# Sinkhorn-sorted attention with a gated MLP: the keys of two batches mixed in 64x64 blocks on four array tiles, and a new order of units

## The chip, the cores and the metric

The kernel runs on one core of a Trainium2 chip. The metric is the device time of one execution in microseconds (us), lower is better. Engines are named as the profile names them: PE is the matrix engine (PEld its weight loads), DVE the vector engine, ACT the scalar engine, POOL the GpSimd engine, SP the engine that here only issues transfers.

## The reference

Four batches of eight heads, 768 tokens, 64 features per head, in float32. An 8x8 matrix per head (`sort_net`) is normalised five times by exp, rows and columns; with it the eight blocks of 96 tokens of k and of v are mixed; each query block attends to its mixed block; then a gated MLP follows.

```python
for _ in range(5):
    P = P - np.max(P, axis=-1, keepdims=True)
    P = np.exp(P)
    P = P / (np.sum(P, axis=-1, keepdims=True) + 1e-09)
    P = P / (np.sum(P, axis=-2, keepdims=True) + 1e-09)
k_sorted = np.einsum('bhij,bhjcd->bhicd', P, k_b).reshape(B, H, S, D)
v_sorted = np.einsum('bhij,bhjcd->bhicd', P, v_b).reshape(B, H, S, D)
...
scores = scale * np.matmul(q_b, k_sb.transpose(0, 1, 2, 4, 3))
attn = softmax(scores)                      # per block of 96 tokens
x = np.matmul(attn, v_sb)                   # heads side by side: (4, 768, 512)
h = np.maximum(x @ w_in, 0.0)               # 512 -> 1024
u, v = h[..., :512], h[..., 512:]
v_n = (v - mu) / np.sqrt(var + 1e-06)
v_s = np.einsum('ts,bsd->btd', w_spatial, v_n) + b_spatial[None, :, None]
out = (u * v_s) @ w_out
```

## The kernel before, in words

The program is straight-line. It is built from small units, and a table of unit names (`ORDER`, L18 to L54) gives the order in which they are emitted; each engine then works through its own instructions in that order and waits at semaphores. A unit's fields are, where they apply, the PSUM bank (a digit from 0 to 3 is a pair of banks, 10 to 17 a single one), the engine that empties the bank (A for ACT, D for DVE, P for POOL), the batch, and the pair of heads or the tile of tokens. Eight banks of PSUM are shared by everything.

The units that matter here:

- `L:q`, `L:k`, `L:v` load one batch of q, k or v, `L:wv`, `L:wu`, `L:wsa`, `L:wsb`, `L:wo`, `BI` load weights and the bias. All are issued by POOL, and the transfers turn float32 into bfloat16. One partition holds six neighbouring tokens of a head, so 128 partitions hold a head.
- `SK` is one round of normalising; `PR` spreads the result over 128 partitions by matmuls (L267); `P0` and `PD` multiply it with a mask to the 128x128 matrix `pd` of each head (P times the identity of 16). `P0` makes the first batch's on DVE, `PD` the others' on POOL, four heads each. There are two buffers of `pd`.
- `KT` mixes and turns the keys of a pair of heads (L395): for each of six strips the keys (128 partitions x 64 features) are the weights and `pd` of the head (128 columns) moves; one head's result goes to the lower 64 partitions of PSUM and the other's to the upper 64. `VT` and `VB` do the like for v of the first batch; `VM` (L422) mixes v of the other batches, and `VC` copies them by transfers into blocks.
- `QT` turns the queries on PE (L326) in the first two batches; in the third and fourth `QP` copies a pair of heads on ACT or DVE (L375) and `QX` turns them by a transfer.
- `SC` (L454) makes the scores of a pair of heads for half of the blocks: 64 rows of the array for each head, then exp on ACT (L459). `AT` (L500) multiplies with the mixed v, and DVE divides (L507, L508). `XT` on PE or `XD` by a transfer (L518) turns the attention's result.
- `VP` and `VH` (L567) make the v half of the hidden layer, `ST`, `LN`, `LA` normalise it; `UP` (L613) the u half; `WT`, `WW` (L536, L543) turn the spatial weights; `SP` and, for the last batch, `SH` (L625, L681) apply them; `GT` and `GH` multiply by u on DVE or POOL; `OP`, `OE`, `OS` and at the end `OH`, `OI`, `OJ` are the output product, its copy out of PSUM and its store.
- `DM` are matmuls on zeros that fill PE's time at the start.

The batches overlap: while one is in the hidden layer, the next is in attention. A second, safe path for inputs out of range stands behind a branch that is not taken here.

Of the kernel before, what the change touches and what calls it, by code (L numbers as in the profile page):

```python
# [8 lines left out]
FP32 = mybir.dt.float32  # L9
# [10 lines left out]
QC:A:0 SK:3 SK:4 QC:A:1 QT:10:A:0:2 IV:2 QT:11:A:0:3 DM:12:4:512 QT:12:A:0:0 DM:13:10:192 PR:10 MB P0:0:2 P0:2:4  # L20
QT:11:D:0:1 VT:2:A:0:0 VT:3:D:0:1 PC:A P0:4:6 P0:6:8 VB:13:A:0:0 VB:12:D:0:1 L:k:0:0:8 VT:2:A:0:2 KT:3:D:0:1
KT:1:A:0:2 KT:0:A:0:3 VT:2:D:0:3 SC:3:0:1:1 KT:1:D:0:0 SC:0:0:2:0 VB:14:D:0:2 SC:3:0:3:0 L:k:1:0:8 AT:1:0:1:1
SC:0:0:0:0 L:v:1:0:8 PD:1:0:4 VB:15:D:0:3 SC:3:0:1:0 AT:1:0:2:0 SC:0:0:2:1 AT:2:0:3:0 SC:3:0:0:1 PD:1:4:8 AT:1:0:0:0
KT:0:A:1:0 XT:14:D:0:0:2 AT:3:0:0:1 SC:1:0:3:1 KT:0:A:1:3 AT:2:0:2:1 VM:1:A:1:0 AT:3:0:3:1 VM:0:A:1:1 VM:2:D:1:3
L:q:1:0:8 VM:1:A:1:2 XT:16:A:0:1:2 L:wv AT:0:0:1:0 XT:17:A:0:1:0 KT:2:D:1:1 KT:1:A:1:2 QT:16:D:1:1 QT:10:D:1:3
QT:11:A:1:2 QT:17:D:1:0 XT:14:D:0:0:0 SC:1:1:1:0 L:wsa SC:0:1:2:1 SC:3:1:2:0 VP:15:D:0:4 ST:0:4 VP:14:D:0:3 L:wu
SC:1:1:0:0 SC:0:1:1:1 VP:15:D:0:1 L:wsb ST:0:3 WT:16:A:1 WT:17:D:0 VP:14:A:0:0 ST:0:1 VH:15:A:0:2 ST:0:0 WT:16:A:2
VC:1:0:4 L:q:2:0:8 VH:17:A:0:5 VC:1:4:8 PD:2:0:4 ST:0:2 ST:0:5 AT:1:1:0:0 LN:0:0:6 AT:0:1:1:0 UP:2:A:0:0:0
UP:3:A:0:1:0 BI LA:0:3 LA:0:4 AT:1:1:2:0 SC:2:1:0:1 UP:0:A:0:1:1 LA:0:1 AT:3:1:2:1 L:v:2:0:8 WT:14:A:3 L:k:2:0:8
LA:0:5 LA:0:2 WW:1:D:4 LA:0:0 SC:0:1:3:1 SC:3:1:3:0 UP:2:A:0:0:1 PD:2:4:8 AT:0:1:3:1 QP:A:2:0 SP:1:0:3 QP:A:2:3  # L30
AT:3:1:3:0 QP:A:2:2 AT:2:1:0:1 QP:A:2:1 SP:0:0:0 AT:1:1:1:1 SP:3:0:2 VM:2:A:2:2 XD:1:0 VM:0:A:2:1 GT:D:0:0 SP:1:0:1
VM:3:D:2:0 GT:P:0:1 VM:2:A:2:3 VH:10:A:1:0 ST:1:0 KT:1:A:2:0 KT:2:D:2:1 KT:3:A:2:3 QX:2:0:4 KT:0:D:2:2 XD:1:1
UP:1:A:1:1:0 VH:16:D:1:1 SC:2:2:2:0 SC:0:2:0:0 VC:2:0:4:0:4 ST:1:1 GT:P:0:2 SC:1:2:3:0 VH:17:D:1:3 L:wo UP:2:A:1:1:1
AT:0:2:2:0 VH:16:A:1:4 AT:1:2:0:0 GT:P:0:3 VH:17:D:1:5 SC:2:2:1:0 L:q:3:0:8 SC:0:2:0:1 SC:1:2:1:1 VH:16:A:1:2 ST:1:3
UP:2:A:1:0:0 ST:1:5 AT:0:2:3:0 ST:1:4 ST:1:2 UP:1:A:1:0:1 LN:1:0:6 OP:3:0:2:2 LA:1:5 LA:1:1 SC:2:2:3:1 L:v:3:0:8
SC:0:2:2:1 PD:3:4:8 LA:1:0 OP:1:0:4:2 PD:3:0:4 LA:1:3 LA:1:2 OE:A:0:2 LA:1:4 L:k:3:0:8 QP:D:3:0 VC:2:4:8:0:4 OE:A:0:4
AT:2:2:3:1 SP:0:1:3 QP:A:3:3 AT:3:2:1:0 AT:1:2:2:1 QP:A:3:1 SP:2:1:1 AT:0:2:1:1 QP:A:3:2 VM:3:A:3:1 OP:1:0:0:2
OE:D:0:0 OS:0:0:0:1:A OS:0:0:1:2:A VM:2:A:3:3 AT:3:2:0:1 SP:0:1:2 VM:1:A:3:0 GT:P:1:1 XD:2:0 VM:3:D:3:2 SP:2:1:0
VH:16:D:2:2 QX:3:0:4 KT:0:A:3:0 KT:1:D:3:2 KT:2:D:3:3 KT:3:A:3:1 XD:2:1 VH:10:D:2:0 SC:1:3:0:1 ST:2:2 SC:3:3:0:0
SC:2:3:3:1 VC:3:4:8:0:4 OS:0:4:0:1 OS:0:4:1:2 VH:11:D:2:4 VH:10:A:2:5 AT:1:3:0:1 GT:P:1:3 VH:16:D:2:3 ST:2:3 ST:2:5  # L40
GT:P:1:2 SC:2:3:1:1 SC:0:3:2:1 SC:1:3:1:0 VH:17:A:2:1 GT:D:1:0 UP:2:A:2:1:0 AT:0:3:2:1 UP:1:A:2:1:1 ST:2:1 AT:3:3:1:1
ST:2:4 AT:2:3:3:1 UP:0:A:2:0:1 ST:2:0 UP:1:A:2:0:0 VC:3:0:4:0:4 AT:3:3:0:0 LN:2:0:6 LA:2:2 OP:0:1:0:2 OE:A:1:0 LA:2:4
AT:2:3:1:0 OP:1:1:4:2 LA:2:5 SC:3:3:2:0 LA:2:0 LA:2:3 LA:2:1 SC:0:3:3:0 OP:2:1:2:2 AT:3:3:3:0 SP:0:2:1 GT:D:2:1
# [25 lines left out]
def kernel(  # L69
# [18 lines left out]
    TB = 128 // NB  # L88
    BH = B * H
# [63 lines left out]
    prep_sb = const.tile([128, NB, BH], BF16, name="prep_sb")  # L153
    vm = const.tile([128, G, H, VW], BF16, name="vm")
# [8 lines left out]
    st = {}  # L163
# [7 lines left out]
    def u_L(what, *a):  # L171
        if what in ("q", "k", "v"):
# [113 lines left out]

    def u_PC(eng):
        copy(eng, prep_sb, st["pr"])
# [157 lines left out]
    def u_SC(ps, b, hp, ih):  # L446
# [3 lines left out]
        for ii in range(NI):  # L450
            i = ih * NI + ii
            for hh in range(2):
                rows = slice(hh * 64, hh * 64 + 64)
# [9 lines left out]
    def u_SM(b, hp, ih):  # L463
# [5 lines left out]
        for ii in range(NI):  # L469
            i = ih * NI + ii  # L470
            for hh in range(2):
                rows = slice(hh * 64, hh * 64 + 64)
# [203 lines left out]
    def u_SH(ps, b, mc, c):  # L676
        b, mc, c = int(b), int(mc), int(c)
        t, x = ps_tile(ps)[:, 0], tokens(c)
        w = x.stop - x.start
        for n in range(G):  # L680
            nc.tensor.matmul(  # L681
                t[:, 0:w], lhsT=st["v_sb", b, n][:, mc * 128:(mc + 1) * 128],
                rhs=wspT[:, x.start // 128:x.stop // 128, n, :],
                start=(n == 0), stop=(n == G - 1),
            )
# [74 lines left out]
    def general_path():  # L760
# [88 lines left out]
```

## Time and profile before

| | |
|---|---|
| time before | 150.09 us, median of 3 runs (149.42 to 150.87) |
| span of the profiled execution, first to last instruction | 147.7 us; its own device time is not given apart, the median of the runs is 2.4 us above its span |
| instructions | 4114 |
| PE / DVE / ACT / POOL busy | 141.4 / 115.1 / 85.2 / 39.1 us |
| first use of the loaded k (first mixing of keys) | 15.45 us |
| first matmul with `wu` (first `UP`) | 38.23 us |
| TensorE clock granted | 1.00 throughout |

A busy time is the union of the instructions of that engine. Times in the views count from the start of the span. In the chain of work that ended last, each piece is the time from the end of the piece before to its own end, so that a delay ahead of a group of matmuls is part of that group's number.

### The profile page before, as it was taken

The numbers are of one execution on the slowest core, as the hardware profiler recorded it, in microseconds if no ns is written. First come the engines' busy times: TensorE is split into PE (matmuls) and PEld (weight loads), VectorE is DVE, ScalarE is ACT, GpSimd is POOL, SyncE is SP. The second block draws the span as 40 slices with busy tenths as digits, with TensorE's granted clock in tenths as the row PEclk, the third lists the DMA queues.
The fourth block names the chain that finished last, engine by engine and source line by source line (L and its number), as shares of the span: only waits on it lengthen the run. The fifth ranks groups of instructions, "written<-read, shape, count | busy, mean of one in ns | idle before, by whom it ended". The sixth has DMA issues, their size and how long they took to land.

```text
span 147.7 us, 4114 instructions
## 1 busy us (share of the span) xinstructions
PE 141.4 (96%) x1691; PEld 101.0 (68%) x1691; DVE 115.1 (78%) x263; ACT 85.2 (58%) x125; POOL 39.1 (26%) x44
## 2 busy tenths in 40 slices
PE   6997999999999999999999999999999999999991
PEld 2466777857776667776877678768866876854760
DVE  3878899979987978867869879899558989846741
ACT  5357998988789447658793328756640046160040
POOL 6701994410000006991002640000002100004630
PEclk9999999999999999999999999999999999999999
DMA  2999999999999999899999999503602507007856
GB/s 60 278 204 205 204 207 201 208 225 243 227 233 231 204 200 269 131 177 211 206 202 175 213 239 278 132 0 83 28 0 60 190 2 284 0 2 266 307 210 228
DMA packets 37013, 25.93 MB, mean 176 GB/s; under 512 B 16704, under 2 KB 34112, under 8 KB 36992
## 3 DMA queue, kind: packets, MB, share of 16 engines
q0 software_dynamic: 14432, 12.19, 51.9%
q1 hardware_dynamic: 21552, 11.88, 33.8%
q10 hardware_dynamic: 1008, 1.57, 2.8%
q8 instruction: 14, 0.23, 0.6%
q14 instruction: 7, 0.06, 0.1%
HBM read 24.78 MB, written 6.29 MB: 210 GB/s over the span
## 4 chain that ended last, share of the span: by engine, by line
PE 82%; DMA 8%; DVE 5%; POOL 2%; issue 1%; ACT 1%; POOLq 0%; DVEq 0%
PE ps L625 16%; PE ps L567 15%; PE ps L613 14%; PE ps L651 11%; DMA k_in<-in_k_dram 8%; PE ps L681 5%; PE ps L500 4%; PE ps L395 4%; PE ps L701 4%; PE ps L454 4%; PE ps L422 3%; DVE x_sb L508 2%; PE ps L326 1%; PE ps L536 1%; PE ps L530 1%; DVE vb L124 1%
## 5 line engine op out<-in xcount | busy, mean ns | idle before, releaser
L642 POOL TENSOR_TENSOR gt<-z,u_sb 128x768 bf16<-128x768 f32 x7 | 11.4, 1642 | 68.0 <-DVE z L631 54.7
L459 ACT ACTIVATE ex_all<-ps 96x768 bf16<-96x768 f32 x32 | 23.7, 805 | 5.0 <-PE ps L454 4.1
L625 PE MATMUL ps<-wspT,v_sb 128*128 128x384 bf16 x144 | 25.0, 326 | 0.0
L567 PE MATMUL ps<-w_in_sb,xT 128*128 128x256 bf16 (+1 forms) x176 | 23.8, 283 | 0.0
L613 PE MATMUL ps<-xT,w_in_sb 128*128 128x384 bf16 x128 | 23.0, 326 | 0.0
L128 ACT ACTIVATE u_sb<-ps 128x768 bf16<-128x768 f32 x16 | 13.0, 811 | 17.3 <-PE ps L613 17.2
L508 DVE TENSOR_TENSOR x_sb<-ps,rec_all 96x512 bf16<-96x512 f32 x32 | 22.0, 687 | 1.1
L625 PEld LDWEIGHTS <-v_sb 128*128 128x128 bf16 x144 | 13.5, 98 | 8.4
L567 PEld LDWEIGHTS <-xT 128*128 128x128 bf16 x176 | 16.2, 98 | 4.0
L651 PE MATMUL ps<-w_out_sb,gt 128*128 128x256 bf16 x144 | 16.9, 273 | 0.0
L613 PEld LDWEIGHTS <-w_in_sb 128*128 128x128 bf16 x128 | 12.0, 98 | 7.0
L587 DVE BATCH_NORM_STATS2 stats<-v_sb 128x6 f32<-128x512 bf16 x24 | 16.2, 675 | 0.6 <-ACT v_sb L128 0.5
L122 ACT COPY o_sb<-ps 128x1024 f32<-128x1024 f32 (+2 forms) x11 | 8.9, 830 | 12.6 <-PE ps L701 9.3
L631 DVE TENSOR_TENSOR z<-ps,b_bc 128x768 f32<-128x768 f32 x12 | 11.5, 954 | 5.9 <-PE ps L625 5.1
L651 PEld LDWEIGHTS <-gt 128*128 128x128 bf16 x144 | 13.8, 98 | 2.0
L500 PEld LDWEIGHTS <-ex_all 96*128 96x128 bf16 x256 | 11.1, 97 | 2.6
L500 PE MATMUL ps<-vb,ex_all 96*128 96x65 bf16 x256 | 12.4, 193 | 0.1
L122 ACT CAST vm<-ps 128x768 bf16<-128x768 f32 x9 | 6.8, 807 | 9.7 <-PE ps L422 6.6
L694 POOL TENSOR_TENSOR gt<-z,u_sb 128x512 bf16<-128x512 f32 (+1 forms) x5 | 5.2, 1046 | 21.5 <-DVE z L687 21.5
L507 DVE RECIPROCAL rec_all<-ps 96x8 f32<-96x8 f32 x32 | 6.3, 196 | 5.5 <-PE ps L500 5.3
L130 DVE TENSOR_SCALAR v_sb<-ps 128x512 bf16<-128x512 f32 (+1 forms) x12 | 8.7, 727 | 1.7 <-PE ps L567 1.5
L236 PE MATMUL ps<-warm 128*128 128x512 bf16 (+3 forms) x38 | 8.5, 386 | 1.3 <-DVE warm L210 1.3
(100 smaller groups left out, 199.9 us busy)
## 6 DMA issues: line engine op xcount, KB each, us to landing
v_in<-in_v_dram POOLq DMA_DIRECT2D x4, 768.0 KB, 16.0
k_in<-in_k_dram POOLq DMA_DIRECT2D x4, 768.0 KB, 14.9
vb<-vm SPq DMA_DIRECT2D x24, 99.0 KB, 4.8
q_in<-in_q_dram POOLq DMA_DIRECT2D x3, 768.0 KB, 11.6
out_dram<-o_sb SPq DMA_DIRECT2D x9, 256.0 KB, 2.3
out_dram<-o_sb SPq DMA_DIRECT2D x4, 512.0 KB, 5.9
out_dram<-o_sb ACTq DMA_DIRECT2D x5, 256.0 KB, 2.3
ws_in<-in_moe_w_spatial_dram POOLq DMA_DIRECT2D x2, 576.0 KB, 18.9
```

Of the source, the lines that this page charges most:

```text
L122: nc.scalar.copy(out=out, in_=in_)
L128: nc.scalar.activation(out=out, in_=in_, func=AF.Relu)
L459: nc.scalar.activation(out=e_tile(b, hp, ih).rearrange("p h (x g) -> p h x g", g=G), in_=t[0:BLK, :, 0:HW].rearrange("p h (g x) -> p h x g ...
L500: nc.tensor.matmul(t[:, hh, ii * VW:ii * VW + D + 1], lhsT=e[:, c:c + 128], rhs=vb[b % 2][:, ih * NI + ii, 2 * hp + hh, 0:D + 1], start=Tr ...
L508: nc.vector.tensor_mul(out=x_sb[:, hp].rearrange("p i (h d) -> p h i d", h=2), in0=tv[:, :, :, 0:D], in1=_raw_ap(rec, 0, [rec.ap[0], [NI, ...
L567: nc.tensor.matmul(t[:, x, c:c + DH // parts], lhsT=st["xT", b][:, n // 3, kc, (n % 3) * 128:(n % 3 + 1) * 128], rhs=w_in_sb[:, kc, DH + c ...
L587: nc.vector.bn_stats(out=stats, in_=st["v_sb", b, n])
L613: nc.tensor.matmul(t[:, x, 0:HW], lhsT=w_in_sb[:, kc, mc * 128:(mc + 1) * 128], rhs=st["xT", b][:, ih, kc, :], start=(kc == 0), stop=(kc = ...
L625: nc.tensor.matmul(t[:, x, 0:HW], lhsT=st["v_sb", b, n][:, mc * 128:(mc + 1) * 128], rhs=wspT[:, 3 * x:3 * x + 3, n, :], start=(n == 0), s ...
L631: nc.vector.tensor_add(out=z.rearrange("p (x c) -> p x c", x=2), in0=t[:, :, 0:HW], in1=b_bc.rearrange("p (x c) -> p x c", x=2),)
L642: eng.tensor_mul(out=gt, in0=st["z", b, mc], in1=u)
L651: nc.tensor.matmul(t[:, x, c:c + w], lhsT=st["gt", b, mc][:, (n0 + x) * 128:(n0 + x + 1) * 128], rhs=w_out_sb[:, mc, c:c + w], start=(mc = ...
```

## The change

The keys of the third and fourth batches (`b >= KB`, KB = 2) are loaded and mixed in another way. A partition holds twelve neighbouring tokens, so a head takes 64 partitions, and two heads stand above each other. The mixing matrix of a head is then 64x64 (`pn`), made by POOL (`PN`) from a second spreading of P (`PS` on PE, `PY` on DVE, with a mask and spread made by POOL in `M8`). One `KP` replaces two `KT`: it mixes two pairs of heads with 48 matmuls of 64 rows, 64 weights and 64 moving columns, and the four that follow each other stand on the four quarters of the array. For odd pairs of heads the two heads change halves (`half`), so `QP` swaps them too, in two copies instead of one. The order of units is new; among other things a few `GT` go from DVE to POOL, three `UP` are emptied by DVE, and most copies of `KT` go to ACT.

```diff
 ORDER = """
...
-VM:3:D:2:0 GT:P:0:1 VM:2:A:2:3 VH:10:A:1:0 ST:1:0 KT:1:A:2:0 KT:2:D:2:1 KT:3:A:2:3 QX:2:0:4 KT:0:D:2:2 XD:1:1
+QX:2:0:4 VM:1:A:2:2 PN:2:0:4 VM:0:A:2:3 GT:D:0:3 GT:P:0:1 UP:2:D:1:0:0 KP:1:0:AD:2:1 VH:16:A:1:2 KP:1:2:AD:2:0
...
+    GR = 2 * G
+    TR = 64 // NB
+    KB = 2
...
     def u_L(what, *a):
-        if what in ("q", "k", "v"):
+        if what == "k" and int(a[0]) >= KB:
...
+            nc.gpsimd.dma_start(
+                out=st["k", b][:, lo:hi],
+                in_=_raw_ap(k, (b * H + 2 * lo) * S * D, [[GR * D, 128], [2 * S * D, hi - lo], [1, GR * D]]),
+            )
...
+    def u_M8():
+        nc.gpsimd.tensor_add(out=mask8, in0=m32[:, 0:TR], in1=m32[:, TR:TB])
+        nc.gpsimd.tensor_copy(out=spread8, in_=spread[:, :, 0:TR])
+
+    def u_PS(ps):
...
+        for i in range(NI):
+            for hh in range(2):
+                nc.tensor.matmul(
+                    parts[hh * 64:hh * 64 + 64, i], lhsT=spread8[:, i * NB:(i + 1) * NB].rearrange("p j t -> p (j t)"),
+                    rhs=turned_p[:, hh, :, KB * HP:], start=True, stop=True,
+                )
...
+    def u_PY(eng):
+        copy(eng, prep8, st["pr8"])
...
+    def u_PN(b, lo, hi):
...
+        nc.gpsimd.tensor_mul(
+            out=pn(b)[:, lo:hi].rearrange("p h (i t) -> p h i t", t=TR),
+            in0=_raw_ap(mask8, 0, [mask8.ap[0], [0, n], [0, NB], [1, TR]]),
+            in1=_raw_ap(prep8, (b - KB) * HP + lo, [prep8.ap[0], [1, n], [(B - KB) * HP, NB], [0, TR]]),
+        )
+
+    def half(b, hp, hh):
+        lo = 64 * (hh ^ (hp & 1) if b >= KB else hh)
+        return slice(lo, lo + 64)
...
     def u_QP(eng, b, hp):
...
+        if half(b, hp, 0).start == 0:
+            copy(eng, to.rearrange("p g h d -> p h g d"), of)
+        else:
+            for hh in range(2):
+                copy(eng, to[:, :, 1 - hh], of[:, hh])
...
+    def u_KP(ps0, ps1, eng, b, m):
+        b, m = int(b), int(m)
+        ts = [ps_tile(ps0), ps_tile(ps1)]
+        for n in range(GR):
+            for row in range(2):
+                g = (n + G * row) % GR
+                for o in range(2):
+                    rows = slice(64 * row, 64 * row + 64)
+                    nc.tensor.matmul(
+                        ts[o][half(b, o, row), g // G, (g % G) * 64:(g % G) * 64 + 64],
+                        lhsT=st["k", b][rows, 2 * m + o, g * D:(g + 1) * D], rhs=pn(b)[rows, 2 * m + o, :],
+                        start=True, stop=True,
+                    )
+        for o in range(2):
+            to = turned("kT", b, 2 * m + o)[:, 0:S].rearrange("p (x b g) -> p b x g", b=2, g=G)
+            copy(eng[o], to, ts[o][:, :, 0:HW].rearrange("p b (g x) -> p b x g", g=G))
...
     def u_SC(ps, b, hp, ih):
...
-                rows = slice(hh * 64, hh * 64 + 64)
+                rows = half(b, hp, hh)
```

Three places show how the order moves.

The first is ACT from the last v of the first batch's hidden layer to the last of that batch's u (`v_sb` and `u_sb` are the copies of `VP`/`VH` and `UP`, `wspT` those of `WT` and `WW`, `rstd` is `LN`, `ex_all` the exp of `SC`). Before:

```order
L122 COPY wspT<-ps 128x768
L128 ACTIVATE v_sb<-ps 128x512
L593 ACTIVATE rstd<-mv,eps 128x6
L594 ACTIVATE rstd<-rstd 128x6
L128 ACTIVATE u_sb<-ps 128x2x384 x2
```

In the change, the same stretch:

```order
L131 ACTIVATE v_sb<-ps 128x512 x2
L125 COPY wspT<-ps 128x768
L131 ACTIVATE u_sb<-ps 128x2x384
L529 ACTIVATE ex_all<-ps 96x768 x2
L131 ACTIVATE u_sb<-ps 128x2x384
L663 ACTIVATE rstd<-mv,eps 128x6
L664 ACTIVATE rstd<-rstd 128x6
```

Of the four `WT`, three stood ahead of the first `UP` before (one of them emptied by DVE, one further up on ACT); now one does, and three come behind it.

The second place is POOL from the first load of k on (`mask_98` and `spread_97` are the two results of `M8`, `pd` is `PD`). Before:

```order
L177 DMA k_in<-in_k_dram 128x8x384 x2
L177 DMA v_in<-in_v_dram 128x8x384
L293 TENSOR_TENSOR pd<-mask_89,prep_sb 128x512 x2
L177 DMA q_in<-in_q_dram 128x8x384
L182 DMA w_in_sb<-in_moe_w_in_dram 128x4x512
L191 DMA ws_in<-in_moe_w_spatial_dram 128x3x768
L185 DMA w_in_sb<-in_moe_w_in_dram 128x4x512
```

In the change:

```order
L302 TENSOR_TENSOR mask_98<-m_88 128x8
L303 COPY spread_97<-spread 32x256
L191 DMA k_in<-in_k_dram 128x8x384 x2
L191 DMA v_in<-in_v_dram 128x8x384
L344 TENSOR_TENSOR pd<-mask_89,prep_sb 128x512 x2
L191 DMA q_in<-in_q_dram 128x8x384
L344 TENSOR_TENSOR pd<-mask_89,prep_sb 128x512 x2
L196 DMA w_in_sb<-in_moe_w_in_dram 128x4x512
L205 DMA ws_in<-in_moe_w_spatial_dram 128x3x768
L199 DMA w_in_sb<-in_moe_w_in_dram 128x4x512
```

Two small operations stand ahead of the loads of k. Of the four `pd` the first and the last are the second batch's, the middle two the third batch's, and one of these stands ahead of the load of q.

The third place is DVE around the mixing of the third batch's keys (`kt_all` are the copies of the mixed keys). Before:

```order
L642 TENSOR_TENSOR gt<-z,u_sb 128x768
L631 TENSOR_TENSOR z<-ps,b_bc 128x768
L124 CAST vm<-ps 128x2x6x64
L587 BN_STATS stats<-v_sb 128x6
L588 BN_AGGR mv<-stats 128x2
L124 CAST kt_all<-ps 128x768 x2
L130 TENSOR_SCALAR v_sb<-ps 128x512
```

In the change:

```order
L701 TENSOR_TENSOR z<-ps,b_bc 128x768
L712 TENSOR_TENSOR gt<-z,u_sb 128x768
L133 TENSOR_SCALAR u_sb<-ps 128x2x384
L127 CAST kt_all<-ps 128x2x64x6 x2
L133 TENSOR_SCALAR v_sb<-ps 128x512 x2
```

DVE keeps two of the four copies, one of each `KP`, and empties an `UP` just ahead of them.

123 lines of the change are left out of this document (73 added, 50 removed).

## The prediction

> **What bounds the kernel now.** I read the page's busy times first, then the busy time by stretches, the first use of each load, and the chain.
>
> ```profile
> PE 141.4 (96%) x1691; PEld 101.0 (68%) x1691; DVE 115.1 (78%) x263; ACT 85.2 (58%) x125; POOL 39.1 (26%) x44
> DMA  2999999999999999899999999503602507007856
> ```
>
> ```profile
> 0.00:15.45 15.45, 12.93 (x143) 7.52 (x144) 10.78 (x46) 8.77 (x15) 6.77 (x15) 1.00 1.05 187
> 15.45:38.23 22.78, 22.31 (x446) 17.35 (x447) 20.78 (x42) 20.93 (x31) 10.15 (x12) 1.00 1.25 216
> 38.23:144.42 106.19, 106.19 (x1109) 76.11 (x1105) 83.27 (x176) 55.46 (x81) 22.16 (x18) 1.00 0.80 164
> ```
>
> The rows give stretch, length, and busy time of PE, PEld, DVE, ACT, POOL. From the first `UP` at 38.23 to the last matmul at 144.42, PE is never idle: 106.19 of 106.19 us. DVE has 83.27 and ACT 55.46 there, and ACT's longest wait in total is for PE (17.2 us, 12 times, the longest 10.9):
>
> ```profile
> ACT u_sb L128 <- PE ps L613: 17.2, 12, 10.9
> ```
>
> So in that stretch each us of PE's work is a us of time. The 3.3 us behind it, to the end of the span at 147.7, are the last copies and stores, whose tail of units is the same after the change. Ahead of it, transfers are busy without a gap (DMA digits of 9 from the second slice on), and the start of the stretch sits close behind a load:
>
> ```profile
> L182 POOL DMA_DIRECT2D w_in_sb<-in_moe_w_in_dram x1: 762/762/762, 17.1 to 17.1; - x1
> DMA to landing us min/median/max: 13.3/13.3/13.3
> ...
> L185 POOL DMA_DIRECT2D w_in_sb<-in_moe_w_in_dram x1: 810/810/810, 18.6 to 18.6; - x1
> DMA to landing us min/median/max: 19.3/19.3/19.3
> ...
> 30.98 1.90 PE L567 MATMUL ps<-w_in_sb,xT 128*128 128x512 bf16 x8
> ...
> 38.23 1.95 PE L613 MATMUL ps<-xT,w_in_sb 128*128 128x384 bf16 x11
> ```
>
> `wv` lands at 17.1 + 13.3 = 30.4, its first matmul starts at 30.98; `wu` lands at 18.6 + 19.3 = 37.9, its first matmul starts at 38.23. Whatever PE saves ahead of 38.23, `UP` can begin at most 0.3 us earlier. The time is then: landing of `wu`, plus PE's sum behind it, plus 3.3.
>
> **PE's sum: what four tiles save, and what changing the tiling costs.** The chain of waits, piece by piece:
>
> ```profile
> 27.34 0.34 PE ps L530 x8
> 34.30 0.67 PE ps L536 x12
> 56.98 1.46 PE ps L395 x48
> 58.44 1.41 PE ps L613 x8
> 59.84 0.87 PE ps L567 x8
> 60.72 0.62 PE ps L454 x24
> 61.34 0.98 PE ps L567 x8
> 62.31 1.30 PE ps L613 x8
> 63.62 0.24 PE ps L500 x8
> 72.03 0.45 PE ps L454 x16
> ```
>
> A matmul on the whole array with 128 moving columns takes 0.67/12 = 56 ns (L536), one with 96 columns 0.34/8 = 42 ns (L530). Mixing keys (L395, 128 columns, half of the array's columns) takes 1.46/48 = 30 ns, scores (L454, 96 columns, half of its rows) (0.62 - 0.45)/8 = 21 ns. So two tiles side by side do run at once, in either direction. Four quarters at once occur nowhere in this trace. 65 moving columns take 0.24/8 = 30 ns (L500).
>
> The same rows show what a border between tilings costs: `VH` takes 0.87, but 0.98 behind the scores; `UP` takes 1.30, but 1.41 behind the mixing; and the scores take 0.62, which is 3 x 0.17 and 0.11 on entering. That is 0.1 us each way.
>
> Per stretch from the first `UP` on:
>
> - Two groups of four `KT` go: 2 x (1.46 + 0.11 behind them) = **-3.14**.
> - Four `KP` of 48 matmuls come. All four quarters at once: 12 rounds of 30 ns (L500's 65 columns) = 0.36 each, **+1.44**. Two at once: 24 rounds, 0.72 each, +2.88. One at a time: 1.44 each, +5.76. The lower end is half of L536's 56 ns a round, 0.33. I take 0.36, since the overlap is seen in both directions.
> - The four `KP` stand in four places, three between `VH` units and one behind `SC`: eight borders, one of which the scores had anyway, so seven or eight; the scores themselves get one visit more, one or two borders. Together I count nine at 0.1: **+0.9**. This is where most of the saving goes back.
> - Two more `WT` stand behind the first `UP` than before; L536's 12 matmuls are two of them: **+0.67**.
>
> The sum is **-0.13 us**. Doing one unit of work with half of PE's time helps little when four units bring eight borders.
>
> [...]
>
> **Ahead of the first `UP`.** From `VP` to `UP` the new order has three `SC` more (3 x 0.17), two borders more and two `WT` less: 0.51 + 0.2 - 0.67 = 0, so 7.25 us as before (30.98 to 38.23). `VP` can't start before 30.4, so `UP` falls between 37.9 and 38.2: **-0.15**, ends -0.3 and 0. `PS` (8 matmuls), `PY` and the mask work fall into the first 15.45 us, where PE is busy for 12.93 with fillers in it and where the load of k decides:
>
> ```profile
> 2.87 0.91 POOL L177 DMA_DIRECT2D v_in<-in_v_dram  x1
> ...
> 4.08 0.36 DVE L221 TENSOR_REDUCE m<-ident 128x16 f32<-128x128 bf16 x1
> ...
> 14.09 2.15 POOL L293 TENSOR_TENSOR pd<-mask,prep_sb 128x512 bf16<-128x512 bf16 x2 [7.56 <-ACT prep_sb L122]
> ...
> 24.19 0.89 POOL L177 DMA_DIRECT2D v_in<-in_v_dram  x1 [1.46 <-DMA v_in<-in_v_dram]
> ...
> DMA to landing us min/median/max: 8.7/16.0/25.7
> ...
> 3.90 11.51 DMA k_in<-in_k_dram
> ```
>
> `M8` waits for DVE's mask until 4.4, so k is issued at some 5.2 instead of 3.90 (two small POOL operations at up to 0.4 each, from `pd`'s 1.1 for 512 elements). v was issued at 2.87 and lands 8.7 later, at 11.5; k queues behind it and lands at 15.4 either way. Price nothing; without that queue it would be 1.3.
>
> On POOL, q of the second batch now stands behind a `pd` that must wait until the first batch's mixing has left its buffer:
>
> ```profile
> 17.30 0.53 PE L395 MATMUL ps<-pd,k_in 128*64 128x128 bf16 x12
> ```
>
> That is near 18. With 1.1 us for each `pd` and 0.9 for the load, q is issued by 20 instead of 16.2, and `wv` to `wu` from 22.2 to 24.5 instead of 17.1 to 18.6. The load ahead of q, the second v, has landed only near 24.0 (POOL's wait in the row at 24.19 ends with it), so the stream does not run dry. Price nothing; the cover is 4 us.
>
> **On the other engines.** `KP`'s two copies are as large as those of `KT` (128x768), split between ACT and DVE. `PN` is half a `pd`, 0.55 us on POOL, behind a `GT`. Before the first `KP`, POOL needs a z (0.95 on DVE), a `GT` (1.64) and `PN`, 3.1 us; PE has between `SP` and `KP` one `AT`, one `SP`, three `VM` and one `UP`, 0.24 + 1.95 + 1.0 + 1.3 = 4.5:
>
> ```profile
> L631 DVE TENSOR_TENSOR z<-ps,b_bc 128x768 f32<-128x768 f32 x12 | 11.5, 954 | 5.9 <-PE ps L625 5.1 <-POOL gt L642 0.9
> L642 POOL TENSOR_TENSOR gt<-z,u_sb 128x768 bf16<-128x768 f32 x7 | 11.4, 1642 | 68.0 <-DVE z L631 54.7 <-DVE rec_all L507 13.2
> ...
> 52.85 0.65 PE ps L422 x4
> ...
> 76.53 0.48 PE ps L500 x16
> 77.02 1.95 PE ps L625 x12
> ```
>
> The cover is 1.4 us. The swapped halves in `QP` cost ACT four more starts of a copy, where it waits 17.2 us for PE's `UP` alone. DVE gives away three `GT`, three copies of v and two of mixed keys and takes three `UP`: less work, where it had 23 us to spare. Several hand-overs (a bank emptied just as `KP` or `SC` wants it) have only a few tenths of slack by such sums; for these I allow +0.3, chosen between 0 (before had none) and 1.
>
> **Sum:** -0.13 - 0.15 + 0.3 = 0.0 us on 147.7; the runs' median lies 2.4 above, so **150.1 us**. No change within 1%, which is about what a measurement of this kernel can tell.
>
> **Rivals.**
>
> - *Two quarters at once, or weights that hold up the rounds.* Weights of 64 columns load for longer than those of 128:
>
> ```profile
> L395 PEld LDWEIGHTS <-k_in 128*64 128x64 bf16 x192 | 5.6, 110 | 1.0 <-issue 0.4 <-DMA k_in<-in_k_dram 0.2
> L500 PEld LDWEIGHTS <-ex_all 96*128 96x128 bf16 x256 | 11.1, 97 | 2.6
> ```
>
> In L395 they hide behind 56 ns of matmul on the same tile; in `KP` only 28 ns are there. If a tile's load needs all 56, a round takes 56 and a `KP` 0.67, as good as two at once (0.72): +1.2 to +1.4, **151.4 us**. Against it: 110 is only 13 above the 97 of L500, whose matmuls follow each other every 30 ns all the same. [...]
>
> - *Slower: the quarters don't run at once at all.* The change would not do what it says; 1.44 for a `KP`, +4.3, **154.4 us**. It decides from a `KP` of 0.8 us on (then the sum passes +1.5). For it: no row has four quarters. Against: pairs overlap both ways. [...]
>
> - *Slower: the last batch's transfers come late.* The last `AT` ahead of the first `XD` of the fourth batch now stands only three `AT` and three `SP` ahead of the `VP` that needs it, 3 x 0.24 + 3 x 1.95 = 6.6 us. In that time DVE adds a z (0.95) and divides (0.2 + 0.69), and the transfer must land:
>
> ```profile
> L508 DVE TENSOR_TENSOR x_sb<-ps,rec_all 96x512 bf16<-96x512 f32 x32 | 22.0, 687 | 1.1
> L507 DVE RECIPROCAL rec_all<-ps 96x8 f32<-96x8 f32 x32 | 6.3, 196 | 5.5 <-PE ps L500 5.3
> ...
> L518 SPq DMA_TRANSPOSE xT<-x_sb x6: 1318/1519/2208, 50.1 to 112.4; - x6
> ...
> DMA to landing us min/median/max: 3.5/4.8/5.7
> ```
>
> 6.6 - 1.85 = 4.75 remain for 3.5 to 5.7: nothing to 1 us late, and if the second one is late as well, 2. It decides from a landing of 6.3 us on; **151.6 us** with 1.5.
>
> - *Faster:* no new wait, rounds of 27 ns, `UP` right at 37.9: -0.13 - 0.14 - 0.3 = -0.6, **149.5 us**. More than that would need `wu` to land earlier.
>
> **How the numbers follow.** Forecast 0.62, two at once or slow weights 0.13, no overlap 0.05, late transfers 0.10, the faster end 0.10. The borders of 1% are 148.6 and 151.6. Slower: half of the two middle rivals (0.12), no overlap (0.05) and 0.04 of the forecast by the scatter of three runs (0.5% either way), 0.21. Faster: 0.02 of the faster end and 0.04 by scatter, 0.06. The rest is 0.73. The range takes the faster end less the runs' scatter, 149.0, and the middle rivals, 152.0; no overlap is left out.
>
> **What would show it.** The weights' first matmul (`UP`) near 38, PE without idle time from there to the end, a `KP` of 0.36 with 0.1 behind it on the next unit, PE's stretch at 106. I would be wrong if `UP` began after 38.5, if a `KP` took 0.7 or more, or if PE stood idle around the first `VP` of the last batch or ahead of a `KP`.

## The result and the profile after

The changed kernel takes **159.29 us** (median of 6 runs, 157.21 to 159.65), the kernel before 150.15 in the same session: 1.0595 times as long, interval 1.0541 to 1.065. Forecast were 150.1, range 149.0 to 152.0. Ratios and intervals leave out executions more than 1.5% above the fastest of their kernel; medians don't. The profiled execution took 159.12 us, its span is 157.3 (before 147.7), so +9.6 are to be explained. All executions here take 1.7 to 1.9 us more than their span; of the 2.4 that the forecast added to the span of before, 0.6 were scatter.

The page of the changed kernel, busy times, then PE's busy share and its granted clock in 40 slices:

```profile
PE 144.0 (92%) x1767; PEld 98.1 (62%) x1767; DVE 112.0 (71%) x258; ACT 87.4 (56%) x131; POOL 46.5 (30%) x52
...
PE   6987999999999999349999999989999999999980
...
PEclk9999999999999999987999999999999999999999
```

PE is at 92% instead of 96%. The loss isn't spread: the digits 3 and 4 stand in two slices (some 63 to 71 us), and from the second of these on the clock shows 8 and 7. Busy time by stretches (length, then busy time of PE, PEld, DVE, ACT, POOL; then granted clock, DMA share, GB/s), the edges set at the first `UP` (38.35) and around the gap:

```profile
38.35:64.08 25.73, 25.68 (x356) 17.28 (x353) 21.32 (x41) 17.36 (x27) 8.58 (x7) 1.00 1.17 190
64.08:69.05 4.97, 0.57 (x11) 0.38 (x8) 0.00 (x0) 1.37 (x2) 3.61 (x5) 1.00 1.11 194
69.05:74.00 4.95, 4.95 (x37) 3.22 (x35) 2.23 (x6) 1.41 (x2) 0.00 (x0) 0.66 1.29 216
74.00:152.81 78.81, 77.91 (x795) 52.76 (x793) 58.19 (x127) 38.05 (x58) 16.94 (x13) 1.00 0.53 129
38.35:152.81 114.46, 109.11 (x1189) 73.64 (x1185) 81.74 (x173) 58.18 (x88) 29.13 (x24) 0.99 0.73 150
```

The 9.6 us, against 106.19 of 106.19 before:

- `UP` starts at 38.35 instead of 38.23: +0.1.
- PE idles 114.46 - 109.11 = 5.35, and 4.4 of it lie between 64.08 and 69.05.
- Behind that gap, 4.95 us run at a mean clock of 0.66: 4.95 x 0.34 = 1.7.
- PE's work itself: 109.11 - 1.7 - 106.19 = +1.2.
- Behind the last matmul 157.3 - 152.81 = 4.5 instead of 3.3: +1.2.

What PE waits for, by the view of waits (us in total, times, longest), and PE's groups in order of time at the gap:

```profile
PE ps L570 <- DMA vb<-vm: 5.1, 3, 2.5
```

```profile
64.08 0.23 PE L570 MATMUL ps<-vb,ex_all 96*128 96x65 bf16 x2
66.17 0.19 PE L570 MATMUL ps<-vb,ex_all 96*128 96x65 bf16 x1 [1.86 <-DMA vb<-vm]
68.90 0.31 PE L570 MATMUL ps<-vb,ex_all 96*128 96x65 bf16 x5 [2.54 <-DMA vb<-vm]
69.05 2.45 PE L683 MATMUL ps<-xT,w_in_sb 128*128 128x384 bf16 x8
71.29 1.77 PE L637 MATMUL ps<-w_in_sb,xT 128*128 128x256 bf16 x8
```

This is one unit, `AT:2:2:1:0`, the third batch's first. Two of its eight matmuls run, the third waits 1.86 us, the fourth 2.54: each for another of the four transfers of `VC:2:0:4` that put the mixed values into `vb`. The `UP` behind takes 2.24 (69.05 to 71.29) instead of 1.30. SP's queue in order of time, after and before (L588 and L518 are `XD`, L435 and L382 `QX`, the last row of each is `VC:2`, eight transfers):

```profile
52.41 5.00 SPq L435 DMA_TRANSPOSE qT<-qp  x1
57.50 1.31 SPq L588 DMA_TRANSPOSE xT<-x_sb  x1
58.90 6.56 SPq L505 DMA_DIRECT2D vb<-vm  x8
```

```profile
51.80 4.27 SPq L382 DMA_TRANSPOSE qT<-qp  x1
56.17 1.32 SPq L518 DMA_TRANSPOSE xT<-x_sb  x1
57.59 5.70 SPq L435 DMA_DIRECT2D vb<-vm  x8
```

`VC` goes out 1.3 us later. In the same microseconds POOL issues the load of w_out. The fourth transfer of `VC:2:0:4` and that load, each with its time from issue to landing, first after, then before:

```profile
L505 SPq DMA_DIRECT2D vb<-vm x1: 572/572/572, 62.2 to 62.2; - x1
...
DMA to landing us min/median/max: 6.6/6.6/6.6
...
L208 POOL DMA_DIRECT2D w_out_sb<-in_moe_w_out_dram x1: 803/803/803, 61.0 to 61.0; - x1
...
DMA to landing us min/median/max: 7.5/7.5/7.5
```

```profile
L435 SPq DMA_DIRECT2D vb<-vm x1: 572/572/572, 59.7 to 59.7; - x1
...
DMA to landing us min/median/max: 3.2/3.2/3.2
...
L194 POOL DMA_DIRECT2D w_out_sb<-in_moe_w_out_dram x1: 817/817/817, 59.8 to 59.8; - x1
...
DMA to landing us min/median/max: 8.9/8.9/8.9
```

Before, the fourth transfer was issued just ahead of the load (59.74 against 59.79 in the trace) and landed after 3.2 us, at 62.95, half a microsecond ahead of its reader. After, it was issued 1.2 us behind the load and landed after 6.6 us, at 68.86, when the load did (68.53). The third transfer went out with the load (both at 60.98 in the trace) and landed after 5.1 us, at 66.12, which is 2.4 ahead of the load: it too was held back (the second, issued ahead of the load, landed after 3.0), but not until the load had landed.

### The profile page after: what moved, and what is told of

It is laid out like the page before. It is cut to its first block, busy times and chain, and to the rows that moved or that the text cites. A ratio compares the mean times of both kernels' runs of the same rounds, so it can differ in the third digit from the quotient of the medians.

```text
span 157.3 us, 4280 instructions
## 1 busy us (share of the span) xinstructions
PE 144.0 (92%) x1767; PEld 98.1 (62%) x1767; DVE 112.0 (71%) x258; ACT 87.4 (56%) x131; POOL 46.5 (30%) x52
## 4 chain that ended last, share of the span: by engine, by line
PE 71%; DMA 15%; DVE 7%; issue 2%; POOL 1%; ACT 1%; DVEq 0%
PE ps L637 14%; PE ps L695 14%; PE ps L683 13%; PE ps L721 9%; DMA k_in<-in_k_dram 7%; DMA vb<-vm 7%; PE ps L570 4%; PE ps L524 3%; PE ps L753 3%; DVE x_sb L578 3%; PE ps L492 2%; PE ps L448 2%; PE ps L773 1%; PE ps L466 1%; DMA out_dram<-o_sb 1%
## 5 line engine op out<-in xcount | busy, mean ns | idle before, releaser
L712 POOL TENSOR_TENSOR gt<-z,u_sb 128x768 bf16<-128x768 f32 x10 | 17.0, 1707 | 76.0 <-DVE z L701 45.9
L683 PE MATMUL ps<-xT,w_in_sb 128*128 128x384 bf16 x128 | 24.5, 336 | 0.0
L131 ACT ACTIVATE u_sb<-ps 128x768 bf16<-128x768 f32 x13 | 10.5, 811 | 21.2 <-PE ps L683 21.0
L637 PEld LDWEIGHTS <-xT 128*128 128x128 bf16 x148 | 14.2, 100 | 6.4 <-issue 0.3
L125 ACT COPY o_sb<-ps 128x1024 f32<-128x1024 f32 (+2 forms) x12 | 10.1, 842 | 12.1 <-PE ps L773 10.8
L131 ACT ACTIVATE v_sb<-ps 128x512 bf16<-128x512 f32 x14 | 8.4, 598 | 5.2 <-PE ps L637 5.1
L766 POOL TENSOR_TENSOR gt<-z,u_sb 128x256 bf16<-128x256 f32 (+1 forms) x6 | 5.5, 944 | 15.2 <-DVE z L759 15.2
```

The lines of the kernel that those rows point to most:

```text
L125: nc.scalar.copy(out=out, in_=in_)
L131: nc.scalar.activation(out=out, in_=in_, func=AF.Relu)
L637: nc.tensor.matmul(t[:, x, c:c + DH // parts], lhsT=st["xT", b][:, n // 3, kc, (n % 3) * 128:(n % 3 + 1) * 128], rhs=w_in_sb[:, kc, DH + c ...
L683: nc.tensor.matmul(t[:, x, 0:HW], lhsT=w_in_sb[:, kc, mc * 128:(mc + 1) * 128], rhs=st["xT", b][:, ih, kc, :], start=(kc == 0), stop=(kc = ...
L712: eng.tensor_mul(out=gt, in0=st["z", b, mc], in1=u)
```

## The experiments

The theory from this (L): a transfer of `VC` that is issued behind a large load is held back by it (some of the expectations below say: until the load has landed, which the third transfer above already contradicts), so the order of issue on two queues decides, not the mixing by blocks. Rivals: K, the mixing costs the time; S, SP is late by itself, whatever else is in flight.

**The load later, in the changed kernel.**

```diff
-VH:12:A:1:3 L:wo GT:P:0:0 AT:0:2:2:0
+VH:12:A:1:3 GT:P:0:0 L:wo AT:0:2:2:0
```

> The load of w_out is issued behind the `GT:P:0:0` that follows it on POOL, 1.7 us later; nothing else changes. Theory L (the transfers `VC:2:0:4` land late because the w_out load is in flight on the same DMA engines): all four are then issued before the load and land about 3 us after their issue, as the first two did (60.32 to 63.28), so the last lands near 64.7; `AT:2:2:1:0` waits about 0.6 instead of 4.7 us, most of the 1.7 us of lower clock behind the gap goes with it, and the kernel takes 153.5 to 155. Rival S (SP's queue is late by itself, whatever else is in flight): the landings and the wait of 4.7 us stay, 159. Rival K (the mixing by blocks costs the time, the wait only shows it): 159 too.

Measured 154.25 us (152.34 to 157.55; ratio to before 1.0235, 1.0089 to 1.0381), clock 0.996. PE at the same place:

```profile
64.28 0.43 PE L570 MATMUL ps<-vb,ex_all 96*128 96x65 bf16 x8
64.54 1.46 PE L683 MATMUL ps<-xT,w_in_sb 128*128 128x384 bf16 x8
```

All eight matmuls run without a wait, and `UP` takes 1.30 again (64.54 to the next unit at 65.84). Exchanging two neighbours on POOL takes some 5 us away (1.0595 to 1.0235; the second interval is wide, but lies below the first); S and K fall as the main cause.

**The same load moved in the kernel before,** without any part of the change, first earlier, then later.

```diff
-ST:1:1 GT:P:0:2 SC:1:2:3:0 VH:17:D:1:3 L:wo UP:2:A:1:1:1
+ST:1:1 L:wo GT:P:0:2 SC:1:2:3:0 VH:17:D:1:3 UP:2:A:1:1:1
```

> The kernel before the change with one thing moved: the load of w_out goes ahead of `GT:P:0:2` on POOL, so that it is issued at about 58.2 instead of 59.8. Theory L (a transfer of `VC` that is issued behind a large load lands only when that load does): before the change the fourth of `VC:2:0:4` was issued at 59.74, 0.05 us ahead of the load, and landed 0.5 us before its reader at 63.45. Now the third and fourth (59.08, 59.74) are behind the load, which takes some 7 us: they land at 65.5 to 66.5, PE waits 2 to 3 us at `AT:0:2:2:0`, the clock dips behind the gap, and the kernel takes 152 to 155, with no part of the change in it. Rival K (the mixing by blocks) and rival S (lateness of SP alone): nothing happens, 150.

```diff
-GT:P:0:2 SC:1:2:3:0 VH:17:D:1:3 L:wo UP:2:A:1:1:1
+GT:P:0:2 SC:1:2:3:0 VH:17:D:1:3 UP:2:A:1:1:1
...
-GT:P:0:3 VH:17:D:1:5
+GT:P:0:3 L:wo VH:17:D:1:5
```

> The kernel before the change with the load of w_out behind `GT:P:0:3`, issued at about 61.5 instead of 59.8. Theory L: the first four transfers of `VC:2` keep their 3 us, the wait stays away with more to spare, and nothing else moves: 149.5 to 150.3. With the loads of the fourth batch 0.8 us later or `OP` waiting for w_out (needed at 70.1, landing near 70) it could lose up to 0.5.

Measured 156.05 (ratio 1.0399, 1.032 to 1.0479) for the earlier load, one microsecond above the range expected, and 149.93 (0.9986, 0.9953 to 1.0019) for the later one. PE with the earlier load:

```profile
64.08 0.19 PE L500 MATMUL ps<-vb,ex_all 96*128 96x65 bf16 x1 [0.42 <-DMA vb<-vm]
66.81 0.19 PE L500 MATMUL ps<-vb,ex_all 96*128 96x65 bf16 x1 [2.54 <-DMA vb<-vm]
67.59 0.31 PE L500 MATMUL ps<-vb,ex_all 96*128 96x65 bf16 x5 [0.58 <-DMA vb<-vm]
67.73 1.75 PE L567 MATMUL ps<-w_in_sb,xT 128*128 128x256 bf16 x8
```

So the old kernel waits 3.5 us at the same place, with the same kind of slow matmuls behind it (mean clock 0.988 in that trace), when the load goes out 1.6 us earlier and nothing else is changed. It had stood at the edge. The second transfer, 0.1 us behind the load, landed 3.3 ahead of it; the third and fourth 0.5 ahead and 0.2 behind.

**The load early, far from `VC`,** in the changed kernel: `L:wo` right behind `L:k:2:0:4`.

> The load of w_out is issued right behind `L:k:2:0:4` on POOL, some 32 us earlier; it then runs behind the third batch's loads and should end near 60 (they end at 55.8, each of this size takes some 4.3 us). Theory L: no load is in flight when the last three of `VC:2:0:4` are issued, the wait at `AT:2:2:1:0` falls from 4.7 us to under 0.5, the clock does not dip, and the kernel takes 152.5 to 153.5. Should loads hold up the transposing transfers on SP as well (`XD:1:0` took 12 us from issue to landing beside `k` of the third batch), then `QX` and `VC` are issued some 3 us later and the wait stays at 2 to 4 us: 155.5 to 158. Rival S without that, and rival K: 159.

Measured 162.3 (160.59 to 163.88), above every range given: of the cases only the second (loads hold up the transposes as well) points that way. SP's queue:

```profile
52.85 6.63 SPq L435 DMA_TRANSPOSE qT<-qp  x1
59.58 1.31 SPq L588 DMA_TRANSPOSE xT<-x_sb  x1
60.98 7.38 SPq L505 DMA_DIRECT2D vb<-vm  x8
```

`QX` now takes 6.63 on SP (5.00 in the changed kernel; 4.4 to 6.0 in the other traces of this order) and `VC` starts at 60.98; the next load on POOL (v of the fourth batch, issued at 63.03) is then ahead of two of its first four transfers, and PE waits 5.2 us for them. So another load ahead of `VC` does the same harm.

**Order alone, mixing alone** (with the load as it was): the new order with `KT` pairs for each `KP`, and the old order with `KP`.

```diff
-KP:1:0:AD:2:1 VH:16:A:1:2 KP:1:2:AD:2:0
+KT:1:A:2:2 KT:0:D:2:3 VH:16:A:1:2 KT:1:A:2:0 KT:2:D:2:1
...
-    KB = 2
+    KB = 4
```

> The new order of units with the old mixing: each `KP` is replaced by the two `KT` of the same half heads, `M8`, `PS`, `PY` and `PN` are left out, `k` is loaded and the query copies `QP` are made as before the change. Theory L (the order brings the wait): the wait at `AT:2:2:1:0` stays, at 3 to 5 us (the unsplit `QP` let `QX` and what is behind it go some 0.5 us earlier), and eight `KT` of 0.39 stand for four `KP` of 0.51, which adds 1.1: 158 to 160.5. Rival K: without `KP` the time falls back to about 150 to 151.5. Rival S: the unsplit `QP` is what was missing on SP, the wait falls below 1 us: 154 to 155.

```diff
-KT:1:A:2:0 KT:2:D:2:1 KT:3:A:2:3 QX:2:0:4 KT:0:D:2:2
+KP:1:2:AD:2:0 QX:2:0:4 KP:3:0:AD:2:1
```

> The old order of units with the new mixing: `KP` in the places of the `KT` pairs of the third and fourth batches, `M8`, `PS`, `PY` and `PN` added beside the first batch's spreading and behind the `PD` of these batches. Theory L: no wait of several us arises; the four `KP` at 0.51 for eight `KT` at 0.39 save about 1.1, and split `QP` and the `PS` matmuls give back 0.4 to 0.8: 149.3 to 150.3. Rival K: the mixing costs several us here as well, 155 to 159. Rival S: the split `QP` makes `QX` and `VC` late by 0.6 us in this order too, so that two or three transfers of `VC:2:0:4` fall behind the w_out load and a wait of 2 to 4 us comes: 152 to 154.

Measured 159.38 (1.0533, 1.0416 to 1.065) for the order alone: within the intervals the whole loss, without `KP`. In its trace (of its longest execution, 162.39) the fourth transfer is issued 0.4 us behind the load, and PE waits 4.2 us for it. The mixing alone in the old order took 164.09 (1.093, 1.0843 to 1.1018), above what any theory gave. SP's rows there:

```profile
52.60 4.09 SPq L435 DMA_TRANSPOSE qT<-qp  x1
56.78 1.31 SPq L588 DMA_TRANSPOSE xT<-x_sb  x1
58.19 7.35 SPq L505 DMA_DIRECT2D vb<-vm  x8
```

`QX` goes out 0.8 us later than before and `VC` 0.6 later. Of the 0.8, 0.3 are the later first `UP` (38.54 for 38.23); the rest goes with the swapped halves, which make `QP` of every second pair two copies of 0.53 instead of one of 0.83. That is enough: the third transfer (60.24) and the fourth (61.47) are now behind the load (60.08), PE waits 3.8 us for them and 4.9 for `vb` in all. So S is part of the truth: a little lateness on SP triggers the wait, and the load sets its size. Another 3.3 us of waiting stand at the end of this kernel (see the old order once more, below).

**The four combinations with the load late** complete this (old order with `KP`, new order with `KT`):

> The old order of units with the new mixing, and the load of w_out behind `GT:P:0:3`. Theory L: the four transfers of `VC:2:0:4` (issued from 58.2 to 61) land by 64.3, the wait of 4.2 us at `AT:0:2:2:0` falls to 0.5 or less and the lower clock behind it goes: 5 to 6.5 us less than the 164.1 with the load where it was, 157.5 to 159. What is left over the kernel before is then in the places seen in that run: 3.3 us ahead of the first `OH`, 1.5 at `AT:1:3:0:1`, 0.8 at `VM:3:D:3:2`. Rival K: no change, 163 to 165.

> The new order of units with the old mixing, and the load of w_out behind `GT:P:0:0`. Theory L: no wait at `AT:2:2:1:0`, about 1 us above the same order with the mixing by blocks (eight `KT` of 0.39 for four `KP` of 0.51), that is 154 to 156, if the wait of 1.2 us for `VC:3` at `AT:2:3:1:1` stays; without it (unsplit `QP`, earlier `QX`) 153. Rival K: 150 to 151.

Measured 158.88 (1.0567, 1.0447 to 1.0688) and 153.37 (1.0211, 1.0108 to 1.0315). The first is as expected. The second is near the 153 expected if the wait for `VC:3` stayed away, and it did; but 1.0 us of waiting came at `AT:2:2:1:0`, where none was expected (the fourth transfer went out 0.04 us ahead of the load and took 4.1). Times as multiples of the kernel before, with intervals:

| | w_out load where it was | load late |
|---|---|---|
| old order, `KT` (before) | 1 | 0.9986 (0.9953 to 1.0019) |
| old order, `KP` | 1.093 (1.0843 to 1.1018) | 1.0567 (1.0447 to 1.0688) |
| new order, `KT` | 1.0533 (1.0416 to 1.065) | 1.0211 (1.0108 to 1.0315) |
| new order, `KP` (after) | 1.0595 (1.0541 to 1.065) | 1.0235 (1.0089 to 1.0381) |

Where the wait arose, the later load takes 0.032 to 0.036 away, some 5 us; where it didn't, nothing. In the new order the two ways of mixing can't be told apart by time.

**How much load is ahead.** In the changed kernel a half, then a quarter of the load stays ahead of `GT:P:0:0`, the rest goes behind it.

```diff
-L:wo GT:P:0:0
+L:wo:0:2 GT:P:0:0 L:wo:2:4
```

> The changed kernel with the w_out load in two: half of it at its place (ahead of `GT:P:0:0`), the other half behind `GT:P:0:0`. Theory L1 (a transfer of `VC` issued behind a load lands when what was issued ahead of it has landed, so that the bytes ahead set the wait): the half takes some 3.8 us in place of 7.5, lands near 65, the third and fourth of `VC:2:0:4` land by 65.5, PE waits 1 to 2 us at `AT:2:2:1:0` in place of 4.7 and the clock falls less: 154.5 to 156.5. Theory L2 (any load in flight slows such a transfer to some 6.5 us, whatever the size of the load): the wait stays above 3.5 us, 158 to 159.5.

> As the kernel with the half, with a quarter of the w_out load at its place and three quarters behind `GT:P:0:0`. L1: the quarter has landed by 63 to 63.5, the fourth transfer of `VC:2:0:4` is bound by its own 3 us and lands near 65.2, the wait at `AT:2:2:1:0` is under 1 us: 153.5 to 155. L2: as with the whole load, 158 to 159.5.

Measured 154.74 (1.0287, 1.022 to 1.0354) and 154.27 (152.97 to 156.52). The waits for `vb`, half and quarter:

```profile
PE ps L572 <- DMA vb<-vm: 2.5, 3, 1.4
```

```profile
PE ps L572 <- DMA vb<-vm: 1.5, 3, 0.7
```

Of these, 0.6 each are at the second place, `AT:2:3:1:1`; for `AT:2:2:1:0` 1.9 and 0.8 are left, the sizes that L1 gave. (With the half, PE also came to the unit 1.1 us later, at 65.14, which shortens its wait.) Landings in the traces: with the half, the load's part at 67.78 and the fourth transfer at 67.61; with the quarter, 65.83 and 65.62; with the whole, 68.53 and 68.86. The fourth transfer lands within 0.4 us of the load ahead of it in three sizes, and L2 is out. L1 as worded isn't shown, though: the third transfer landed 0.9 us ahead of the half, and with the quarter the fourth took 3.8 us, within what transfers take with no load ahead. The two parts took 6.4 and 4.4 us to land, more than the 3.8 and 2 expected; whether the transfers slow the load as well wasn't tested.

Fourteen traces have the load of w_out undivided and near `VC:2`, and together they show more exactly how far the order of issue goes with the landing. Transfers issued ahead of the load took 2.7 to 4.1 us to land; 0.1 to 0.5 us behind it, 4.4 to 7.7; further behind it, 5.7 to 9.1; at the same instant (0.01 to 0.03 us behind) it went either way, 2.8 to 5.1.

How a load on one queue holds back a small transfer on another, no run here shows.

**The second wait.** In the fourth batch the half that is read first was sent last; the late load, and `VC:3:4:8` ahead of `VC:3:0:4`:

> The changed kernel with the load of w_out behind `GT:P:0:0` (as in the first of these experiments, 154.25) and the two halves of `VC:3` in the other order: `VC:3:4:8` goes first. The first `AT` of the fourth batch (`AT:2:3:1:1`) reads that half and waited 1.2 us for its last transfer, issued 94.67 and landed 98.53. Theory L, second place (what is read first was sent last): the half is issued 2.6 us earlier, the wait of 1.2 us goes and no new one comes (`AT:3:3:3:0`, the first reader of the other half, is some 6 us later): 152.8 to 153.4. Rival: the transfers are slow for another reason, or `AT:3:3:3:0` waits in its place: 154 to 154.5.

Measured 152.93 (1.0192, 1.0131 to 1.0253), within the range expected. In the trace the wait at that place is gone; it had been 0.9 us, the other 0.3 of the 1.2 stood in an earlier batch. The two times alone, with intervals 1.0131 to 1.0253 and 1.0089 to 1.0381, can't be told apart. PE's longest wait left in the second half is 0.9 us for w_out, the late load itself. PE's stretch there, from the first `UP` to the last matmul:

```profile
38.59:146.99 108.40, 107.07 (x1187) 73.02 (x1185) 81.78 (x173) 58.23 (x88) 29.11 (x24) 1.00 0.79 158
```

**The same with `KT`,** to price the mixing once no transfer of `VC` is late:

> The new order of units with the old mixing, and with both waits for `VC` mended (the w_out load behind `GT:P:0:0`, `VC:3:4:8` first), beside 152.9 for the same with the mixing by blocks. It tells what the mixing itself is worth where no transfer is late. If the saving of the matmuls counts (eight `KT` at 0.39 take 3.1, four `KP` at 0.51 take 2.0): 153.5 to 154.5. If the split query copies, `PS` and the borders between tilings give it back: 152.3 to 153.3.

Measured 154.3 (1.023, 1.0166 to 1.0295), which overlaps 1.0131 to 1.0253. By time this is inconclusive: the mixing is worth little more than 1% at most, either way. PE's busy time from the first `UP` to the last matmul says more. With the late load it is 108.00 with `KT` and 107.22 with `KP`, so in this order the blocks save 0.8 us of PE's work; in those two traces a first `UP` 0.3 later and a tail 0.9 longer hide it.

**The clock behind the gap.** Twenty matmuls on constants into the bank of `AT:2:2:1:0`, ahead of it (`DM:14:20:512 AT:2:2:1:0`), in the changed kernel:

> The changed kernel with 20 matmuls of 512 columns on constant data into the bank of `AT:2:2:1:0`, ahead of it: TensorE works some 4.3 us while it waits for `VC:2:0:4`. Theory G (1.7 us of the loss are the lower clock after an idle stretch): `UP:3:A:1:0:1` takes 1.30 instead of 2.24 and `VH:12` 0.88 instead of 1.60, the granted clock stays above 0.99, and the kernel takes 157 to 158. Rival: the slow matmuls behind the gap have another cause (the transfers that are landing): 159 to 160.

Measured 156.68 (1.0452, 1.0417 to 1.0487), clock 1.00:

```profile
64.51 4.48 PE L250 MATMUL ps<-warm 128*128 128x512 bf16 x19
68.83 0.54 PE L570 MATMUL ps<-vb,ex_all 96*128 96x65 bf16 x3
71.07 0.31 PE L570 MATMUL ps<-vb,ex_all 96*128 96x65 bf16 x5 [1.70 <-DMA vb<-vm]
71.22 1.47 PE L683 MATMUL ps<-xT,w_in_sb 128*128 128x384 bf16 x8
```

The transfers land no earlier, but `UP` takes 1.30 again: work without a use saved 0.0143 of the time before, 2.1 us, as expected (the median is 0.3 us below the range). In the changed kernel the slow piece has a length of its own:

```profile
69.37:72.78 3.41, 3.41 (x15) 1.91 (x13) 1.62 (x4) 0.81 (x1) 0.00 (x0) 0.50 1.29 218
```

The clock is granted at 0.50 for 3.41 us and at 1.00 on both sides, so 1.7 us are lost. The two idle pieces ahead of it were 1.86 and 2.54 long, and the one matmul between them (0.19 us) didn't keep the clock up.

**The old order with `KP`, once more.** Its runs had 3.4 us of waiting at the branch that ends the usual path (`tc.If`). Two kernels: the start's fillers cut finer (`DM:13:60:32` for `DM:13:10:192`), which adds 100 instructions; and that with two mends (one query copy with a negative step, `PS` and `PY` elsewhere). The author's estimate for the first, if the place of the branch in the code is what makes it slow: the branch falls to under 0.6, the 3.4 us of waiting and the lower clock behind it go, 153.5 to 155.5.

> The old order with the new mixing and the late w_out load (158.9), with 60 warm-up matmuls of 32 columns instead of 10 of 192 at the start: the same columns, but 100 more instructions of TensorE ahead of the branch that ends the usual path. There TensorE's branch took 4.9 us, and 0.4 to 0.5 in the other kernels. [...] Rival (the blocks' mixing or POOL's lateness makes it): 158 to 160. [...]

> As the kernel before this one in the list, with two more things mended: the swapped query copies `QP` are one copy with a negative step instead of two (2 x 0.53 against 0.83 us on ACT, twice a batch), so that `QX` and `VC` go out 0.4 us earlier; and `PS` writes another bank, `PY` goes behind `VB:15` on DVE, which takes 0.6 us of waiting out of the first batch's spreading. Theory: 0.6 from the start, 0.4 to 0.8 from the waits for `VC`, so 1 to 1.5 under the kernel with the longer code alone: 152.3 to 154.3. If the mixing by blocks were worth what its matmuls save (0.9 us), the kernel would come out at 149 to 150, below the kernel before.

Measured 154.76 (1.0305, 1.0245 to 1.0366) and 155.32 (1.0393, 1.033 to 1.0456). PE's branch instruction (ns), first without, then with the longer code:

```profile
L894 PEldq COMPARE_BRANCH  x1: 4904/4904/4904, 141.1 to 141.1; - x1
```

```profile
L894 PEldq COMPARE_BRANCH  x1: 392/392/392, 141.4 to 141.4; - x1
```

So 4 us of that kernel's loss (1.0567 to 1.0305) went with 100 instructions more ahead of the branch; that its place in the code is the reason, and not the finer fillers as such, is argued, not shown. The mends were a miss: the query copy is one of 0.83 again, but `PY` only moved its 0.8 us of waiting from `VB` to the first scores, and k of the first batch came 0.9 late. `KP` in the old order stays 4.5 to 6 us above the kernel before; none of these versions beats it. What is left there isn't matmul time: with the longer code PE is busy 106.25 us from the first `UP` on, as before (106.19). The first `UP` comes 1.2 later, PE waits 3.1 in pieces of 1.0 and less, and the tail is 0.9 longer.

## Why the prediction was wrong

**What held.** `UP` starts at 38.35 (forecast 37.9 to 38.2, "wrong if after 38.5"), but not by the landing of `wu`: that came at 37.58, and PE had `AT` units to run until 38.35. In the trace of before, too, PE was busy up to 38.23. So PE's own order sets this start, and the landing is only a bound. PE's order up to 64.08 runs without a wait to speak of, 25.68 busy of 25.73. All four quarters run at once:

```profile
58.30 0.58 PE L466 MATMUL ps<-pn,k_in 64*64 64x64 bf16 x48
58.81 1.05 PE L637 MATMUL ps<-w_in_sb,xT 128*128 128x256 bf16 x8
```

From the start of `KP` to that of the next unit are 0.51 us; forecast were 0.36 and 0.1 for the border. Two at once (0.72) and none at once (1.44) are out, and with them the two rivals: 48 matmuls in 0.51 us start 11 ns apart. None of PE's waits behind 38.35 is for `M8`, the order on POOL or `PN`. The last batch's transposes weren't late.

**The step that failed** is the one on the other engines, "Several hand-overs ... have only a few tenths of slack by such sums; for these I allow +0.3". It summed slack for PE's, POOL's and DVE's hand-overs, but did not follow SP's queue except for the last batch's `XD`: neither the copies of `QP` through `QX` to `VC`, nor what else is in flight when `VC` is issued. One of those hand-overs was 4.4 us of idle PE and 1.7 of lower clock behind it, and a second one 0.7 (`AT:2:3:1:1`). The trace of before had it all: the fourth `VC` 0.05 us ahead of the load, landing 0.5 us ahead of its reader, and the next four `VC` transfers, issued behind the load, landing after 6.5 to 7.7 us. A rival "`VC` falls behind the load" at 3 to 5 us of wait (6.5 to 8.9 of landing, the load's own being the longest, less the 3.2 and the 0.5 of slack) would have stood at 153 to 155.

**A term mis-sized.** PE's sum was to be -0.13. With both waits gone PE is busy 107.07 instead of 106.19, so +0.9. Counting each matmul in the two traces up to the start of the next, the terms that were summed came out: the mixing -0.9 (2.06 for 2.93, without the borders behind it; forecast -0.8 with them) and the transposes of the spatial weights +0.6 (forecast +0.67). What the sum put at nothing came to some +1.2: the last output product +0.4, `SP` +0.3, `UP`, `AT` and `SH` +0.2 each, `SC` +0.1, less 0.3 in the v half and `VM`. In the new order with `KT` and the late load most of this is there as well, so it belongs to the order; why these units take longer there is open. The tail behind the last matmul was forecast unchanged and is 4.5 us instead of 3.3. There the last store took 3.1 us to land instead of 1.9; in the run with the fillers, with the same units, it took 2.1 and the tail was 3.4, so the units aren't the reason. The best version of the new order has a span 3.1 us longer than before: 0.4 ahead of `UP`, 0.9 of PE's work, 1.3 of waits (0.9 of them for w_out) and 0.6 of tail (3.8 us).

**The conditions named as proof of error** (`UP` after 38.5, `KP` from 0.7, idle PE around the last `VP` or ahead of a `KP`) all stayed away, and the result lay 7 us outside the range. They guarded only what had been summed. The sign that did fail is the one named for being right, PE without idle time from 38 to the end: it idled 5.35 us.

## What to carry to other kernels

Where the bounding engine has no idle time, list every transfer it reads, with its issue, its landing and the start of its reader, and ask what else is issued in the same microseconds on any queue; half a microsecond of slack beside a load of 512 KB was an edge here, not a cover (the fourth `VC` landed after 3.2 us when it was issued 0.05 ahead of the load, after 6.6 when it was issued 1.2 behind it). When such a kernel is reordered, first move the load out of the way of the small transfers, since a wait of 4.4 us cost 1.7 more by the clock here. And change one thing at a time: order, mixing and 100 instructions more ahead of a branch each moved this kernel by more than the gain that was sought.

## What was not expected of the hardware

- A 99 KB transfer took 2.7 to 4.1 us to land when it was issued ahead of a load of 512 KB on another engine's queue, and 5.7 to 9.1 when it was issued more than 0.5 us behind it. In the trace of before, two neighbouring ones were issued 0.6 us apart, one just ahead of the load and one behind it: they took 3.2 and 6.5 us.
- With one more load ahead, the transposing `QX` held SP for 6.63 us, against 4.4 to 6.0 in the other traces of this order. This is one run.
- Two idle pieces of 1.86 and 2.54 us with one matmul between them were followed by 3.41 us at half the clock. The mean clock of that trace is 0.989. In the run with half of the load, with pieces of 1.36 and 0.58 at the same place, it is 0.993; with `KT` and both mends, where the longest wait was 1.9 us for w_out, it is 0.989 again. So the length of a wait alone doesn't decide it here.
- One branch of TensorE took 4.9 us, and 0.4 with 100 instructions more ahead of it. What holds it, no trace here shows.
